# How far apart the loads of k, q and v are paced, from the third batch on

## The chip, the cores and the metric

The kernel runs on one core of one Trainium2 chip. The metric is the device time of one execution in microseconds. A core has a matmul engine (TensorE, PE in the profile, with its weight loads as PEld), VectorE (DVE), ScalarE (ACT), GpSimd (POOL) and SyncE (SP), which here only issues DMA transfers. Each engine runs its own list of instructions in order and waits on semaphores for the others. A DMA transfer is issued by one engine and carried out by 16 DMA engines that the core has to itself.

## The reference

Two blocks follow each other. The first is attention without a softmax, with a norm at the end; the second sends each token to one of eight experts.

```
# B, H, S, D = 8, 8, 576, 64
kv  = einsum('bhsd,bhse->bhde', k, v)
o   = einsum('bhsd,bhde->bhse', q, kv)
rms = sqrt(mean(o * o, axis=-1) + 1e-6)
x   = (o / rms * g_norm)  ->  (B*S, H*D) = (4608, 512)

# 8 experts, 576 tokens each
logits = x @ w_gate                      # (4608, 8)
# (token, expert) pairs by falling logit; a pair is taken if the token
# is still free and the expert not yet full
out[mask_e] = relu(x[mask_e] @ w1[e]) @ w2[e]     # w1 (512, 1024), w2 (1024, 512)
```

All inputs and the output are float32.

## The kernel before, in words

**Attention.** The work goes batch by batch, eight of them. k, v and q of a batch (576 rows of 64 for each of eight heads) are loaded in two halves each, so a batch has six loads of 576 KB, and the kernel has 48 in all. `load` (L82) makes a tile for one half, with a tag such as `k0` or `q1` that has two buffers, and hands the DMA to `paced`. A load of batch b + 2 therefore needs the buffer that batch b used, and waits until TensorE has read it for the last time.

`prepare(b)` (L368) turns a batch's loads into what attention needs. `sum_kv(r)` (L392) multiplies k with v for two heads at a time and adds up over the rows; `sum_kv(0)` and `sum_kv(1)` use the first halves of k and v, `sum_kv(2)` and `sum_kv(3)` the second. `turn_q(n)` (L376) transposes four blocks of q on TensorE; n = 0, 1, 2 use the first half of q, n = 2, 3, 4 the second. As soon as the last reader of a half has been written down, `again` (L399) writes down the load of the same half for batch b + 2.

`tiles` (L466) and its function `one` (L477) multiply the turned q with kv, 128 tokens at a time, take squares on ScalarE and sum them on VectorE. `logits` (L513) has GpSimd scale the tokens into `xo`, and collects writes of `xo` to a DRAM array `x_dram`, 20 of them, in the list `writes`.

The loop at L546 goes over the batches: between the output tiles of batch b it puts the pieces of `prepare(b + 1)`. Batches with an odd number have five output tiles, the others four. On TensorE, VectorE, ScalarE and SyncE the order is the order written down (`manual_schedule`, L542), so SyncE's list is: the 12 loads of the first two batches (L91), then the loads of the later ones as `again` writes them down, then the writes. The writes of the first six batches come after all the loads, at the ends of rounds 4 and 5 of the loop. The others follow after the last round; their `xo` is made by ScalarE in a list called `late`.

**Pacing.** `paced` (L74) keeps a list of all DMAs it has been handed, loads and writes together, numbered here from 0: 0 to 5 are the first batch's, 12 to 17 the third's, 42 to 47 the eighth's, 48 to 67 the writes. It adds a dependency to each: the DMA waits until the one three places ahead of it in this list has landed.

**Routing and experts.** After attention, VectorE and TensorE search for the thresholds that fill the first expert (`threshold`, L653). SyncE then reads the expert's number (L905), loads its weights (L911, L913), and GpSimd gathers its tokens from `x_dram` (L966). `turn` (L1047) and `layers` (L1090) do the matrix products, and the searches for later experts run beside them.

Of the kernel before, what the change touches and what calls it, by code (L numbers as in the profile page):

```python
# [26 lines left out]
def kernel(  # L27
# [14 lines left out]
    B, H, S, D = q.shape  # L42
# [25 lines left out]


    loaded = {}  # L70
    AHEAD = 3
    issued = []

    def paced(dma):  # L74

        if len(issued) >= AHEAD:
            tc.add_manual_dep(dma.ins, issued[-AHEAD].name,
                              mybir.DependencyInfo(mybir.DependencyClass.Sync, mybir.DependencyReason.DATA),
                              reason="paced loads")
        issued.append(dma.ins)  # L80

    def load(name, b, h):  # L82

        loaded[name, b, h] = att.tile([P, NP // 2, R, D], FT, name=f"{name}_sb", tag=name + str(h), bufs=2)
        rs = slice(h * NP // 2, (h + 1) * NP // 2)
        src = {"k": k, "v": v, "q": q}[name]
        paced(nc.sync.dma_start(
            loaded[name, b, h].rearrange("p r j d -> p r (j d)"),
            src[b].rearrange("h s d -> (h s) d").rearrange("(r p j) d -> p r (j d)", r=NP, j=R)[:, rs]))
# [138 lines left out]
    for st in range(1, NSTEP):  # L228
        n = (1.0 + 2 * FUZZ) / (NCAND + 1) if 1 < st <= DIGITS else 1.0 / (NCAND + 1)
# [4 lines left out]
    for st in range(1, NSTEP):  # L234
        n = (1.0 + 2 * FUZZ) / (NCAND + 1) if st <= DIGITS else 1.0 / (NCAND + 1)
# [230 lines left out]
    def tiles(c0, rows):  # L466
# [46 lines left out]
        def logits():  # L513

            part = att.tile([P, T * H, E], FT, name="part", tag="part")
            nc.vector.tensor_tensor(
                part, o_sb[:, :, :, D:W].rearrange("p t h e -> p (t h) e"),
                inv.rearrange("p (a o) -> p a o", o=1).to_broadcast([P, T * H, E]), op=AL.mult)
            nc.vector.reduce_sum(out=lg[:, :, c0:c0 + T].rearrange("p e t -> p t e"),
                                 in_=part.rearrange("p (t h) e -> p t e h", t=T), axis=AXX)  # L520

            for t in range(T):
                if own:
                    nc.gpsimd.tensor_tensor(xo[:, t], o_sb[:, t, :, 0:D],  # L524
                                            inv[:, t * H:(t + 1) * H].rearrange("p (h o) -> p h o", o=1).to_broadcast([P, H, D]),
                                            op=AL.mult)
                else:
                    for h in range(H):
                        late.append(lambda t=t, h=h: nc.scalar.mul(xo[:, t, h], o_sb[:, t, h, 0:D],
                                                                   inv[:, t * H + h:t * H + h + 1]))  # L530
            for x in range(0, T, 2):
                y = min(x + 2, T)
                writes.append(lambda x=x, y=y: paced(nc.sync.dma_start(
                    x_dram[(c0 + x) * P:(c0 + y) * P, :].rearrange("(t p) f -> p t f", p=P),
                    xo[:, x:y].rearrange("p t h d -> p t (h d)"))))
# [55 lines left out]
    for nm, shape in (("row", (NCAND + 1,)), ("cut", (2, GC)), ("mx", (GC,)), ("code_mx", (GC,)), ("mine", (GC,)),  # L591
                      ("shut", (E,)), ("code", (E,)), ("one_more", (3,)), ("marks", (NCAND // 2,)), ("which", (1,)), ("over_room", (E,)), ("last", (E,)), ("last_one", (1,)), ("begin", (1,)), ("half", (NB,)),
                      ("rise", (2, GC))):
        n = shape[0] * (shape[1] if len(shape) > 1 else 1)
# [6 lines left out]
    for nm, shape in (("n", (E, G)), ("all", (3, E)), ("a", (GC + 2,)), ("s", (NB, GC + 3))):  # L601
        n = shape[0] * (shape[1] if len(shape) > 1 else 1)
# [737 lines left out]
```

## Time and profile before

| | us |
|---|---|
| median of 3 runs | 644.92 (644.12 to 647.33) |
| profiled execution | 645.28 |
| its span, first to last instruction | 643.5 |
| TensorE busy | 600.3 (93%) |
| VectorE busy | 379.4 (59%) |
| GpSimd busy | 385.4 (60%) |
| ScalarE busy | 201.6 (31%) |
| first expert's weight load issued | 139.83 |

Times inside the profile are counted from the span's start. A row of the timeline gives start, duration, engine, line, operation, the tiles written and read, and how many instructions were merged; what stands in brackets is the idle time of the engine before it and what ended it. "issue" there means that the engine waited for nothing that the profile shows. The engine names with a q at the end, such as SPq, are sequencers: what they show of a DMA is its issue, not its travel. Queue 1 in the DMA table carries SyncE's transfers, queue 0 GpSimd's gathers and scatters, and queues 8 and 14 are of kind "instruction". The granted clock is the share of TensorE's full clock that the chip allowed in a stretch of time.

Attention takes about the first 106 us, the search for the first expert runs to about 140, and the eight experts fill the rest. DMA moves 305 GB/s between 20 and 94 us.

### The profile page before, as it was taken

Reading aid. Unit: us, or ns where it says so; the run is one execution under the profiler, and the core shown is the slowest. Engines: PE = TensorE matmul, PEld = TensorE weight load, DVE = VectorE, ACT = ScalarE, POOL = GpSimd, SP = SyncE. Lnnn points to the kernel's source line nnn. Section 1 sums busy time; section 2 is a strip of 40 time slices with the busy share of each in tenths; the row PEclk is TensorE's granted clock in tenths of the full one; section 3 lists DMA queues with packets and bytes.
Section 4 is the critical chain, followed back from the end, with each engine's and each line's share of the span. In section 5 each row is a group of like instructions: output and inputs, shape, how many; then the busy total and the mean of one; then the engine's idle time right before and its main releaser. Section 6 shows DMA issues by size and latency. Waiting matters only on the chain.

```text
span 643.5 us, 12772 instructions
## 1 busy us (share of the span) xinstructions
PE 600.3 (93%) x4914; PEld 465.6 (72%) x4924; DVE 379.4 (59%) x1242; ACT 201.6 (31%) x429; POOL 385.4 (60%) x402
## 2 busy tenths in 40 slices
PE   8889998348999999999999999999999999999994
PEld 4778887325787778677867786778678777867873
DVE  4457768776796778489658857966661062032101
ACT  1556666913221232213122312231232213122310
POOL 1136534005865697489729873887498579749822
PEclk9989999559999999999999999999999999999998
DMA  8899999438018107210911181027105410910001
GB/s 270 293 305 301 306 318 359 168 116 263 7 49 303 58 2 280 89 42 1 329 39 42 42 295 41 34 77 259 58 17 167 179 63 1 325 51 34 1 10 65
DMA packets 49853, 91.03 MB, mean 141 GB/s; under 512 B 3712, under 2 KB 20096, under 8 KB 49792
## 3 DMA queue, kind: packets, MB, share of 16 engines
q1 hardware_dynamic: 43200, 71.31, 32.4%
q0 software_dynamic: 5888, 18.88, 8.6%
q8 instruction: 39, 0.64, 0.4%
q14 instruction: 22, 0.18, 0.1%
q10 hardware_dynamic: 704, 0.02, 0.1%
HBM read 71.32 MB, written 18.87 MB: 140 GB/s over the span
## 4 chain that ended last, share of the span: by engine, by line
PE 79%; DVE 7%; issue 5%; DMA 4%; ACT 2%; POOL 1%; POOLq 0%; SPq 0%; DVEq 0%; ACTq 0%
PE x_ps L1156 13%; PE x_ps L1116 12%; PE z_ps L1156 9%; PE y_ps L1156 9%; PE y_ps L1116 8%; PE z_ps L1116 7%; PE o_ps L492 5%; PE y_ps L1218 4%; DMA v_sb<-in_v_dram 3%; PE qt_ps L381 3%; PE t_ps L1058 3%; PE kv_ps L396 2%; PE given_ps L670 1%; DMA q_sb<-in_q_dram 1%; PE given_ps L665 1%
## 5 line engine op out<-in xcount | busy, mean ns | idle before, releaser
L1161 ACT COPY h<-x_ps 128x288 f32<-128x288 f32 x93 | 37.2, 400 | 166.1 <-PE x_ps L1156 159.8
L1156 PE MATMUL x_ps<-xs,sw 128*128 128x288 f32 x248 | 71.4, 409 | 0.4 <-DVE xs L1071 0.4
L1083 POOL DMA_INDIRECT out_dram<-y_sb,outs x32 | 31.4, 983 | 56.7 <-DVE y_sb L1254 41.1
L1116 PE MATMUL x_ps<-tw,sh 128*128 128x256 f32 x256 | 61.5, 384 | 0.0
L1156 PEld LDWEIGHTS x_ps<-xs,sw 128*128 128x128 f32 x248 | 46.1, 190 | 13.4 <-issue 1.0
L1063 ACT ACTIVATE xt<-t_ps,g_col 128x512 f32<-128x512 f32 (+3 forms) x41 | 25.8, 635 | 91.4 <-PE t_ps L1058 91.2
L1108 POOL TENSOR_TENSOR sh<-hid 128x512 f32<-128x512 f32 x32 | 40.6, 1270 | 19.8 <-ACT hid L1131 19.8
L1116 PEld LDWEIGHTS x_ps<-tw,sh 128*128 128x128 f32 x256 | 47.0, 190 | 7.0 <-issue 0.8
L1044 POOL TENSOR_TENSOR sw<-w_sb 128x256 f32<-128x256 f32 x64 | 46.7, 730 | 7.8 <-PE z_ps L1156 7.4
L1131 ACT ACTIVATE hid<-hid 128x576 f32<-128x576 f32 x64 | 43.8, 686 | 22.5 <-DVE hid L1170 12.5
L524 POOL TENSOR_TENSOR xo<-o_sb,inv 128x512 f32<-128x512 f32 x27 | 28.3, 1079 | 34.1 <-DVE inv L511 34.1
L966 POOL DMA_INDIRECT xg<-x_dram,ids x40 | 38.1, 952 | 15.6 <-issue 10.4
L1194 POOL TENSOR_TENSOR tw<-w_sb 128x512 f32<-128x512 f32 x32 | 40.0, 1270 | 6.8 <-DMA w_sb<-in_moe_w_dram 6.8
L492 PE MATMUL o_ps<-kvx,qt 64*128 64x72 f32 (+1 forms) x640 | 39.9, 272 | 2.7 <-ACT o_sb L499 1.6
L492 PEld LDWEIGHTS o_ps<-kvx,qt 64*128 64x128 f32 (+1 forms) x640 | 34.9, 178 | 8.2 <-issue 5.1
L1156 PE MATMUL z_ps<-xt,sw 128*128 128x288 f32 x128 | 38.0, 414 | 0.0
L1156 PE MATMUL x_ps<-xt,w_sb 128*128 128x288 f32 x124 | 37.3, 415 | 0.5 <-ACT xt L1063 0.5
L1156 PE MATMUL y_ps<-xt,w_sb 128*128 128x288 f32 x128 | 36.8, 408 | 0.0
L1156 PE MATMUL z_ps<-xs,sw 128*128 128x288 f32 x128 | 36.8, 409 | 0.0
L1156 PE MATMUL y_ps<-xs,w_sb 128*128 128x288 f32 x128 | 36.5, 407 | 0.0
L503 DVE TENSOR_REDUCE ms<-sq 128x8 f32<-128x512 f32 x36 | 24.5, 683 | 19.8 <-ACT sq L498 19.7
L1248 ACT COPY u<-x_ps 128x512 f32<-128x512 f32 x24 | 14.0, 584 | 66.3 <-PE x_ps L1116 52.6
(306 smaller groups left out, 1322.1 us busy)
## 6 DMA issues: line engine op xcount, KB each, us to landing
w_sb<-in_moe_w_dram SPq DMA_DIRECT2D x32, 512.0 KB, 5.3
w_sb<-in_moe_w_dram SPq DMA_DIRECT2D x8, 2048.0 KB, 13.1
k_sb<-in_k_dram SPq DMA_DIRECT2D x16, 576.0 KB, 5.8
v_sb<-in_v_dram SPq DMA_DIRECT2D x16, 576.0 KB, 5.6
q_sb<-in_q_dram SPq DMA_DIRECT2D x16, 576.0 KB, 6.1
x_dram<-xo SPq DMA_DIRECT2D x16, 512.0 KB, 4.1
x_dram<-xo SPq DMA_DIRECT2D x4, 256.0 KB, 2.9
xg<-x_dram,ids POOLq DMA_INDIRECT x40, 5.2
```

The lines of the kernel that those rows point to most:

```text
L492: nc.tensor.matmul(o_ps[rows_at, rp, (2 * r2 + l) * W:(2 * r2 + l + 1) * W], lhsT=turned_q[bn][ks, l, block // 2:block // 2 + m].rearrange ...
L524: nc.gpsimd.tensor_tensor(xo[:, t], o_sb[:, t, :, 0:D], inv[:, t * H:(t + 1) * H].rearrange("p (h o) -> p h o", o=1).to_broadcast([P, H, D ...
L966: tokens = nc.gpsimd.indirect_dma_start(out=xg[0:nr], out_offset=None, in_=x_dram, in_offset=bass.IndirectOffsetOnAxis(ap=ids[0:nr, n:n + ...
L1044: in_order(nc.gpsimd.tensor_tensor(o, x, y, op=op))
L1063: nc.scalar.mul(xt[:, :, a + c:a + d], t_ps[:, :, c:d], g_col)
L1083: put = nc.gpsimd.indirect_dma_start(out=out, out_offset=bass.IndirectOffsetOnAxis(ap=ids_of[t][0:nr, n:n + 1], axis=0), in_=y_sb[0:nr, :] ...
L1108: in_order(nc.gpsimd.tensor_tensor(o[:, ms], x[:, ms], y[:, ms], op=op))
L1116: nc.tensor.matmul(p_ps[:, n], lhsT=left[:, f, n * P:(n + 1) * P], rhs=right[:, f], start=first, stop=(f == FH - 1), skip_group_check=True)
L1131: nc.scalar.activation(both, both, ACT.Relu)
L1156: nc.tensor.matmul(p_ps, lhsT=lhs[:, r], rhs=rhs[:, r], start=(m in (1, 2, 4, 5) and r == 0), stop=(r == 1), skip_group_check=(m in (6, 7, ...
L1161: nc.scalar.copy(u, p_ps)
L1194: in_order(nc.gpsimd.tensor_tensor(o, x, y, op=AL.subtract))
```

## The change

`paced` takes its distance from the place in the list. For numbers 12 to 47, the loads of the third to the eighth batch, it is six places; for the first 12 loads and for the writes it stays three.

```diff
     loaded = {}
-    AHEAD = 3
+    AHEAD, APIECE = 3, 6
     issued = []

     def paced(dma):

-        if len(issued) >= AHEAD:
-            tc.add_manual_dep(dma.ins, issued[-AHEAD].name,
+        n = APIECE if 2 * APIECE <= len(issued) < B * APIECE else AHEAD
+        if len(issued) >= n:
+            tc.add_manual_dep(dma.ins, issued[-n].name,
                               mybir.DependencyInfo(mybir.DependencyClass.Sync, mybir.DependencyReason.DATA),
                               reason="paced loads")
         issued.append(dma.ins)
```

Lines after this one have numbers that are one higher in the changed kernel.

## The prediction

> **What bounds the kernel now.** I read the page first (busy shares, the chain of waits), then TensorE's waits and timeline inside the attention stage, then SyncE's DMA issues, then the clock and the DMA rows stretch by stretch. The page's chain:
>
> ```profile
> span 643.5 us, 12772 instructions
> PE 79%; DVE 7%; issue 5%; DMA 4%; ACT 2%; POOL 1%; POOLq 0%; SPq 0%; DVEq 0%; ACTq 0%
> ```
>
> DMA has 4% of the chain, about 26 us, and the page puts three quarters of it on one v load group. The merged chain shows these pieces all before 26.3 us: loads of v at 1.25, 7.87 and 12.68, and a load of q at 19.24 that lands at 26.17. After that TensorE carries the chain through attention. So the question is what loads do to TensorE after about 21 us, where the changed loads begin. TensorE's waits from 18 to 110 us:
>
> ```profile
> PE kv_ps L396 <- issue: 3.9, 3, 1.6
> ...
> PE o_ps L492 <- issue: 0.7, 1, 0.7
> PE qt_ps L381 <- DMA q_sb<-in_q_dram: 0.2, 1, 0.2
> ```
>
> Columns are microseconds in total, times, longest. TensorE waits 0.2 us for a load and 4.6 us for "issue", that is for nothing the profile can name. Its timeline places these:
>
> ```profile
> 25.05 1.03 PE L396 MATMUL kv_ps<-v_sb,k_sb 64*64 64x64 f32 x47 [1.08 <-issue]
> 26.30 0.63 PE L381 MATMUL qt_ps<-ident,q_sb 128*128 128x128 f32 x4 [0.22 <-DMA q_sb<-in_q_dram]
> ...
> 37.84 1.70 PE L396 MATMUL kv_ps<-v_sb,k_sb 64*64 64x64 f32 x59 [1.56 <-issue]
> ...
> 61.89 0.67 PE L492 MATMUL o_ps<-kvx,qt 64*128 64x72 f32 x8 [0.66 <-issue]
> ...
> 84.80 0.35 PE L396 MATMUL kv_ps<-v_sb,k_sb 64*64 64x64 f32 x9 [1.28 <-issue]
> ```
>
> They fall in the middle of a run of matmuls on tiles already in use, and between the stops at 23.97 and 36.28 I count 252 matmul records, between 36.28 and 61.23 about twice that. This is the pace at which TensorE's instructions are fetched: queue 8 is of kind "instruction", 39 packets of 0.64 MB, 16 KB each, two to such a stretch. I take the stops for late instruction blocks. They are the only thing after 26.3 us that the loads could still change.
>
> The loads themselves, by SyncE's issues:
>
> ```profile
> 19.24 1.87 SPq L87 DMA_DIRECT2D q_sb<-in_q_dram  x2
> 22.68 0.37 SPq L87 DMA_DIRECT2D k_sb<-in_k_dram  x1
> 26.18 0.37 SPq L87 DMA_DIRECT2D v_sb<-in_v_dram  x1
> ...
> 30.70 3.45 SPq L87 DMA_DIRECT2D q_sb<-in_q_dram  x2
> 35.28 0.37 SPq L87 DMA_DIRECT2D k_sb<-in_k_dram  x1
> ...
> 93.53 37.42 SPq L533 DMA_DIRECT2D x_dram<-xo  x20
> ```
>
> Loads are numbered from 0 here, six to a batch. Load 12 (k of the third batch) goes at 22.68, load 18 at 35.28; each issue also shows that the load three places back has landed. So load 13 (v) had landed by 30.70 and is first read at 33.48, and load 15 (second half of v) had landed by 35.28 and is first read at 35.83: 0.55 us to spare, the thinnest margin. For later batches the same reading gives 3.4 to 6 us (fourth batch: v landed by 42.76, read at 49.09; eighth: landed by 88.92, read at 94.90). Loads are paced, but nobody waits for them.
>
> Clock and DMA by stretch (columns: busy time and count of the five engines, granted clock, DMA share, GB/s):
>
> ```profile
> 20.00:94.00 74.00, 67.18 (x1565) 58.46 (x1573) 46.91 (x140) 45.13 (x89) 30.55 (x34) 0.98 0.92 305
> 38.00:40.00 2.00, 2.00 (x62) 1.88 (x59) 0.00 (x0) 0.42 (x1) 0.13 (x1) 0.56 0.89 277
> ...
> 196.00:204.00 8.00, 8.00 (x47) 6.87 (x46) 5.25 (x19) 0.59 (x1) 6.58 (x8) 1.00 1.05 384
> ```
>
> **The change, part by part.** No instruction is added or removed, the order on every engine is the same, and on PE, ACT, DVE and POOL the waits are too. On SyncE the waits of 36 loads (12 to 47) move from three places back to six, and three writes behind them get an extra landing to wait for.
>
> 1. SyncE's own waits. Between 20 and 94 us it waits 56.4 us for landings (21.3 + 20.0 + 15.1) and 4.1 us for TensorE to free buffers. Most of the 56.4 goes and waits for buffers take its place. What is queued behind a waiting load is the next load, then 20 writes, then the weight loads, which need a routing result near 139.8 us. Nobody on the chain waits there: 0 us. What is late next is the buffer: each tile name has two buffers, so load 47 can't go before the sixth batch's last q tiles have been turned, about 81.6 us in the timeline.
>
> 2. A faster load stream. With up to 5 transfers queued (weights, 196 to 204 us, gathers beside them) the queues moved 384 GB/s at a share of 1.05, against 305 at 0.92 now. The 36 loads are 21.2 MB: 70 us at 305, 55 at 384; the buffers hold it to about 60. The last load goes at 82 to 86 us rather than 92. TensorE waits 0.2 us for loads in all, so the value is between 0 and -0.2 us; I take 0.
>
> 3. The q loads of the second batch. Loads 12, 13 and 14 no longer wait for a landing (the places six back, 6 to 8, had to land for 9 to 11) and their buffers are free by about 14 us; they go right behind load 11, at some 21.1 to 21.9 us instead of 22.68, 26.18 and 27.70. Load 10, the q load on the chain, is still on its way then. If they take bandwidth from it, 26.17 moves later, straight onto the chain. Ends: -0.2 us (the wait at 26.30 goes) and +3.5 us (one more of the largest gap between landings, 22.68 to 26.18). The nearest row is the five weight loads issued at 188.85 to 191.35: the small ones land in 6.2 us at the median, the large one in 15.6. The early ones were not held to the last one's time, so I take +0.3 us.
>
> 4. The late instruction blocks, 1.08 + 1.56 + 0.66 + 1.28 = 4.58 us, and the clock. After the 1.56 us stop the clock falls to 0.56 (38 to 40 us): 59 records take 1.70 us where 72 take 1.38 elsewhere (+0.57), four turns 1.11 instead of 0.66 (+0.45), an output tile 1.64 instead of 1.11 (+0.53), 1.55 us in all. Ends: the three stops after 26 us and the dip go, -(1.56 + 0.66 + 1.28 + 1.55) = -5.1 us; or refills stretch as the one in this row, from 21 to 24 us, did:
>
> ```profile
> q8 instruction: 1, 0.02, 4.8%
> ```
>
> There 4.8% of 16 engines times 3 us is 2.3 us for one 16 KB block, where other windows give 2.1%, 1.0 us. That is +1.3 us for each of three stops, +3.9. Which end? Two 3 us windows in the expert stage, one with the queues empty but for the block, one with them full:
>
> ```profile
> DMA packets 1, 0.02 MB, mean 5 GB/s; under 512 B 0, under 2 KB 0, under 8 KB 0
> ...
> q8 instruction: 1, 0.02, 2.3%
> ```
>
> ```profile
> DMA packets 467, 1.12 MB, mean 375 GB/s; under 512 B 40, under 2 KB 40, under 8 KB 466
> ...
> q8 instruction: 1, 0.02, 2.3%
> ```
>
> A block takes 1.1 us in both (231 to 234 and 255 to 258 us). The size of the queue beside it does not set its time, so the stops stay: 0 us.
>
> A rule that speaks against this change is in the Trainium skill, "DMA: Bandwidth & Descriptors", section on latency and other measured facts: access to HBM takes 0.2 us on average and 2 us under high load. If six loads in flight were the high load and three were not, each of the three late blocks would cost 1.8 us more, an estimate of +5.4 us from that page. The rows just shown do not have it: full and empty queues give the same block time.
>
> 5. The 20 writes start with the load stream's end, some 6 to 10 us earlier. The last five wait for ACT's late copies and the gathers for routing (first at 143.69 us), so the end stays: 0 us. Were that cover gone, the cost would be a landing, 4.1 us at the median.
>
> Sum: 0 + 0 + 0.3 + 0 + 0 = +0.3 us. The profiled execution took 645.28 us (span 643.5 and 1.8 around it), 0.36 above the median of the three runs, 644.92. Against the median: 645.2 us. Half a percent, 3.2 us, is about what a measurement of this kernel can tell from no change; the three runs lie that far apart.
>
> **The rivals.**
> Slower: a deeper queue delays instruction blocks, at the stops of 36, 61 and 84 us. For it: the 2.3 us block at 21.42, while loads were in flight. Against it: the pair of windows above. Price +1.3 us for each stop, and 1.55 us if one more of them makes the clock fall: +3.9 to +5.5, 649 to 651 us. It decides from the third stretched block (or two and a dip, 4.2 us) on.
> Faster: from about 45 us the loads wait for buffers, queues run empty between them, blocks come sooner. For it: a stop of 1.56 us only just cost the clock, so a slightly shorter one saves the 1.55 us as well. Against it: a block takes 1.1 us even alone. Price -3.1 us (36 us stop with its dip) to -5.1: 640 to 642 us. It needs the dip to go.
> Nothing moves: the stream is held by something other than the pace and still runs at 305 GB/s; the last load stays near 92 us. For it: a share of 0.92 leaves little. Against it: 384 GB/s later. Time 644.9, inside the forecast.
>
> **How the numbers follow.** Forecast (within 3.2 us of before, the third rival included) 0.57; slower by refills or by the q load of step 3 0.23; faster 0.20. The slower side gets more since step 3 can only add. The range goes from the faster rival's lower price, 640, to the slower's upper, 651, since each tail holds about 2 in 10; the likeliest case's own range is 642 to 648. Chances: faster 0.20, within 0.57, slower 0.23.
>
> **What would show it.** Step 1: SyncE's waits for landings fall below 25 us between 20 and 94 us and waits on PE grow. Step 2: the last load goes before 87 us, with 330 GB/s or more from 21 to 45 us. Step 3: the turn after the second batch's kv sums starts at 26.3 to 26.6 us. Step 4: 3 to 5 "issue" stops on TensorE, 3.5 to 5.5 us together, at the same matmul counts. Step 5: writes start at 84 to 88 us and end near 131. The prediction is wrong if TensorE's stops vanish or double, if a clock dip comes or goes, or if the routing after 106 us shifts by more than attention did.

## The result and the profile after

The changed kernel is slower: a ratio of 1.0076 to the kernel before, 95% interval 1.0048 to 1.0104. The ratio leaves out executions more than 1.5% above the fastest of their kernel, two of the changed kernel's 17, so it is not the quotient of the medians that follow. The median of 17 executions is 651.31 us, that of the kernel before 646.58 us in the same comparison, 4.7 us less. The profiled execution of the changed kernel took 648.27 us, with a span of 646.5 us against 643.5 before.

The page's span and chain, after:

```profile
span 646.5 us, 12770 instructions
PE 77%; DVE 9%; issue 6%; DMA 4%; POOL 1%; ACT 1%; POOLq 0%; SPq 0%; DVEq 0%; ACTq 0%
```

"issue" grew from 5% to 6% of the chain. These rounded shares of the whole span do not say where: up to 108 us the chain holds about 1.5 us more of it than before. TensorE's waits from 18 to 110 us, after (microseconds in total, times, longest):

```profile
PE kv_ps L397 <- issue: 4.8, 3, 2.5
PE o_ps L493 <- issue: 1.4, 2, 1.1
PE kv_ps L457 <- issue: 0.6, 1, 0.6
```

No wait for a load is left in this list. The "issue" waits at the kv sums (L397) and output tiles (L493) went from 4.6 to 6.2 us. TensorE's timeline, after, at the same instructions as those shown of before:

```profile
24.32 1.03 PE L397 MATMUL kv_ps<-v_sb,k_sb 64*64 64x64 f32 x47 [0.26 <-issue]
25.50 0.63 PE L382 MATMUL qt_ps<-ident,q_sb 128*128 128x128 f32 x4
...
38.03 1.59 PE L397 MATMUL kv_ps<-v_sb,k_sb 64*64 64x64 f32 x59 [2.48 <-issue]
...
42.94 1.97 PE L382 MATMUL qt_ps<-ident,q_sb 128*128 128x128 f32 x8
...
64.09 0.67 PE L493 MATMUL o_ps<-kvx,qt 64*128 64x72 f32 x8 [1.08 <-issue]
...
87.03 0.35 PE L397 MATMUL kv_ps<-v_sb,k_sb 64*64 64x64 f32 x9 [2.10 <-issue]
```

The stops are at the same records: after 25, 13, 8 and 60 matmuls of the same groups. The one near 24 us is shorter (0.26 for 1.08), the other three are longer by 0.92, 0.42 and 0.82 us. That is 5.9 us for the four, 4.6 before; the rest of the 6.2 is a wait of 0.36 us at 45.26, while the clock is low. The eight turns at 42.94 take 1.97 us, where they take 1.09 at full clock. The clock after the long stop, and DMA over the stage, after:

```profile
20.00:94.00 74.00, 66.53 (x1530) 57.92 (x1535) 45.46 (x135) 43.37 (x86) 30.55 (x34) 0.95 0.96 340
...
38.00:40.00 2.00, 1.97 (x61) 1.85 (x62) 0.00 (x0) 0.34 (x1) 0.00 (x0) 0.64 1.05 389
40.00:42.00 2.00, 2.00 (x18) 1.67 (x16) 0.72 (x6) 0.83 (x2) 0.85 (x2) 0.50 1.08 398
42.00:44.00 2.00, 2.00 (x15) 1.88 (x14) 0.69 (x1) 1.37 (x3) 0.36 (x1) 0.50 1.03 381
```

From 25 to 45 us, before and after:

```profile
25.00:45.00 20.00, 17.73 (x363) 15.23 (x365) 11.57 (x53) 9.72 (x20) 6.61 (x8) 0.91 0.91 298
```

```profile
25.00:45.00 20.00, 16.99 (x313) 14.32 (x307) 11.08 (x48) 9.50 (x19) 6.60 (x8) 0.84 1.05 391
```

DMA moves 340 GB/s instead of 305 from 20 to 94 us, and 391 instead of 298 from 25 to 45. The clock's dip lasts about 7 us instead of 3.4. TensorE's first search matmul begins at 115.26 instead of 113.25 us, which is 2.0 of the 3.0 us by which the two spans differ. From there to the first weight load it is 26.6 us in both; the other 1.0 us is in the expert stage, and no experiment followed it.

SyncE's issues, after:

```profile
20.51 0.47 SPq L88 DMA_DIRECT2D k_sb<-in_k_dram  x1
21.02 0.77 SPq L88 DMA_DIRECT2D v_sb<-in_v_dram  x1
21.84 0.90 SPq L88 DMA_DIRECT2D k_sb<-in_k_dram  x1
...
80.13 3.27 SPq L88 DMA_DIRECT2D q_sb<-in_q_dram  x2
85.46 47.49 SPq L534 DMA_DIRECT2D x_dram<-xo  x20
```

Loads 12 to 14 go at 20.5 to 21.8 us and the last load by about 83. Up to 45 us the stream runs ahead; from 52 us on each load goes when its buffer comes free.

### The profile page after: what moved, and what is told of

Its sections match the earlier page's. It is cut to its first block, busy times and chain, and to the rows that moved or that the text cites. A ratio compares the mean times of both kernels' runs of the same rounds, so it can differ in the third digit from the quotient of the medians.

```text
span 646.5 us, 12770 instructions
## 1 busy us (share of the span) xinstructions
PE 601.2 (93%) x4914; PEld 466.7 (72%) x4924; DVE 380.2 (59%) x1242; ACT 201.6 (31%) x429; POOL 385.5 (60%) x402
## 4 chain that ended last, share of the span: by engine, by line
PE 77%; DVE 9%; issue 6%; DMA 4%; POOL 1%; ACT 1%; POOLq 0%; SPq 0%; DVEq 0%; ACTq 0%
PE x_ps L1157 13%; PE x_ps L1117 11%; PE z_ps L1157 9%; PE y_ps L1157 9%; PE y_ps L1117 8%; PE z_ps L1117 7%; PE o_ps L493 4%; PE y_ps L1219 4%; PE qt_ps L382 3%; PE t_ps L1059 3%; DMA v_sb<-in_v_dram 3%; PE kv_ps L397 2%; PE given_ps L671 1%; DMA q_sb<-in_q_dram 1%; PE given_ps L666 1%
## 5 line engine op out<-in xcount | busy, mean ns | idle before, releaser
L493 PE MATMUL o_ps<-kvx,qt 64*128 64x72 f32 (+1 forms) x640 | 40.3, 273 | 2.5 <-issue 1.4
L493 PEld LDWEIGHTS o_ps<-kvx,qt 64*128 64x128 f32 (+1 forms) x640 | 35.2, 180 | 8.2 <-issue 5.8
L504 DVE TENSOR_REDUCE ms<-sq 128x8 f32<-128x512 f32 x36 | 24.4, 683 | 21.9 <-ACT sq L499 21.8
```

The source lines that it names most:

```text
L493: nc.tensor.matmul(o_ps[rows_at, rp, (2 * r2 + l) * W:(2 * r2 + l + 1) * W], lhsT=turned_q[bn][ks, l, block // 2:block // 2 + m].rearrange ...
```

## The experiments

Three theories stood at the start. A: the load stream makes TensorE's next instruction block come late, and more so with six loads ahead. B: the loss comes from the later batches, whose loads now wait for buffers. C: the clock dips fall by chance and the loads have no part in it.

**Half of the change each.** The condition on the number in the list is cut:

```diff
-        n = APIECE if 2 * APIECE <= len(issued) < B * APIECE else AHEAD
+        n = APIECE if 2 * APIECE <= len(issued) < 4 * APIECE else AHEAD   # early_six
+        n = APIECE if 4 * APIECE <= len(issued) < B * APIECE else AHEAD   # late_six
```

> Six places ahead for the loads of the third and fourth batch only (12 to 23), three for all others. Theory A (a deeper queue of loads makes TensorE's next instruction block start later, and the stop near 36 us with the clock dip behind it grows): nearly all of the loss is here, 3 to 5 us slower than before, a stop of 2.2 to 2.7 us near 36 us and a dip of two clock windows (6.8 us). Theory B (the loss comes from the later batches, whose loads now wait for buffers and are issued in bursts tied to TensorE): 0 to 1 us slower, the 36 us stop back near 1.6 us. Theory C (the clock dips fall by chance and the queue has no part in it): within 2 us of before, and the stop near 36 us is anything from 1.2 to 2.6 us.

> The other half: three places ahead up to load 23, six for loads 24 to 47 (fifth to eighth batch). Theory A: the stop near 36 us is 1.4 to 1.7 us with one clock window at half as before; the stops near 62 and 85 us grow by 0.3 to 0.8 us as in the changed kernel only if many loads are in flight then; 0 to 1.5 us slower than before. Theory B: 3 to 5 us slower, with the growth in the stops near 62 and 85 us. Theory C: within 2 us of before.

Measured: the early half alone 1.0067 (1.0042 to 1.0091) of before, median 648.85 us; the late half alone 1.0056 (1.0034 to 1.0079), 648.29 us. Each half costs nearly what both cost, so A and B as worded both fall short: the late half was to cost 0 to 1.5 us by A and the early half 0 to 1 by B. The traces give a part of the reason. With the late half alone the stream runs ahead at 43 to 67 us instead, and there the stop near 60 us is 1.75 us, against 0.66 and 1.21 in two profiles of before. The profile of the early half alone is of its longest execution, 656.91 us, so it does not show where the median's loss lies. Its long stop is the one near 24 us:

```profile
26.28 1.75 PE L397 MATMUL kv_ps<-v_sb,k_sb 64*64 64x64 f32 x47 [2.23 <-issue]
27.96 1.11 PE L382 MATMUL qt_ps<-ident,q_sb 128*128 128x128 f32 x4
```

The windows of the same profile (busy time and count of the five engines, clock, DMA share, GB/s):

```profile
28.00:42.00 14.00, 14.00 (x151) 10.83 (x154) 7.20 (x32) 5.90 (x12) 3.04 (x4) 0.50 1.05 391
```

The clock stays at half for 14 us and more, with TensorE never idle. What follows one stop can cost far more than the stop. The 16 KB instruction block that ends this one travelled 2.75 us, against about 1.0 for most; near 36 us, with TensorE at half clock and 391 GB/s moving, there was no stop at all.

**The stops are instruction blocks.** The 18 warm-up matmuls at the start become 36 of half the width, with six ahead and with three:

```diff
-        ones(18)
+        ones(36, width=256)
```

(`ones` gets a parameter for the width in both kernels; its lines are left out here.)

> The changed kernel, with the 18 warm-up matmuls at the start split into 36 of half the width: the same time on TensorE, 36 instructions more. If the stops are late instruction blocks (theory A and B), every stop moves forward by 18 matmul records in TensorE's order: the one near 36 us from record 13 of the second half's kv sums to the output tile before it, where matmuls take three times as long, so it shrinks from 2.5 to about 1.5 to 2.0 us; the one near 85 us from record 60 of the first half's sums to record 42 and stays near 2 us. The time falls by 0 to 3 us against the changed kernel. Theory C, or stops that come from data or semaphores: they stay at the same matmuls.

> The kernel before with the same split of the warm-up matmuls. Theories A and B: the stop near 36 us moves into the output tile ahead of the second half's kv sums and shrinks from 1.56 to 0.5 to 1.2 us, too short to cost the clock a window, so the dip (1.55 us) goes as well: 1 to 3 us faster than before. Theory C: stops at the same matmuls and no change.

Measured: 1.0025 (0.9999 to 1.0052), 647.04 us with six; 0.9986 (0.9951 to 1.0022), 644.91 us with three. The stops moved as counted. With six ahead:

```profile
24.49 1.27 PE L397 MATMUL kv_ps<-v_sb,k_sb 64*64 64x64 f32 x65 [0.62 <-issue]
...
34.23 0.89 PE L493 MATMUL o_ps<-kvx,qt 64*128 64x72 f32 x11
37.83 0.71 PE L493 MATMUL o_ps<-kvx,qt 64*128 64x72 f32 x5 [2.71 <-issue]
```

and with three:

```profile
34.12 0.89 PE L492 MATMUL o_ps<-kvx,qt 64*128 64x72 f32 x11
36.37 0.45 PE L492 MATMUL o_ps<-kvx,qt 64*128 64x72 f32 x5 [1.37 <-issue]
```

65 records are left at the first stop where 47 were, and the second stop falls after 11 of the 16 records of the output tile, 18 records ahead of where it was. Later stops moved by 18 as well: the one near 61 us (1.14 us with three ahead, 0.18 with six), and with three ahead also one at 65.60 and one at 88.02 us, which lie 18 records ahead of stops at 70.09 us in the third profile of the changed kernel and at 94.13 us in the second of before; with six there is one at 96.42, at the same instruction as the one at 88.02. The one expected near 85 us is in neither profile. A wait for data or a semaphore would have stayed with its instruction, so the places are set by the count of TensorE's instructions.

The DMA records of the traces say the same. Between 20 and 100 us the 17 profiles of this document have 67 stops marked "issue" of 0.2 us or more, and 63 of them end 1.2 to 1.55 us after a 16 KB block of queue 8 has landed. The other four are of 0.36 us each, while the clock is at half.

The sizes were not as expected: 2.71 us with six (1.5 to 2.0 expected), 1.37 with three (0.5 to 1.2), and with three ahead the time did not fall by the 1 to 3 us expected. At the same place, six ahead costs 1.34 us more, in one profile each; the one with six is of that kernel's longest execution, 654.32 us.

**No load stream.** The third and later batches use the tiles of the first two again:

```diff
+    kept = dict(loaded)
...
-                    load(name, b + 2, h)
+                    loaded[name, b + 2, h] = kept[name, b % 2, h]
```

> The kernel before without its loads 12 to 47: the third and later batches use the first two batches' k, q and v again, so what is computed from them is other data. Nothing else is left out. Theory A (the queue of loads delays instruction blocks): with almost empty queues from about 25 us on, the stops near 36, 61 and 84 us fall to 0 to 0.6 us each, no clock window at half before 110 us, 4 to 7 us faster than before. Rival (an instruction block is late in a short stretch of matmuls whatever the queues do): stops of 1.0 to 1.6 us stay, 0 to 2 us faster.

Measured: 0.9904 (0.9876 to 0.9931), 639.19 us. TensorE's waits from 18 to 100 us:

```profile
PE kv_ps L457 <- issue: 0.6, 1, 0.6
PE kv_ps L397 <- issue: 0.5, 1, 0.5
PE qt_ps L382 <- DVE qt L386: 0.2, 1, 0.2
PE ones_ps L362 <- issue: 0.2, 1, 0.2
```

Both "issue" waits of half a microsecond are before 25 us, when the last of the 12 loads is still on its way. After that there is no stop up to 93 us, and the clock is not lowered before 104 us. This is theory A's expectation: the loads make the blocks late, with three ahead as well. Theory C is out in so far as it gives the loads no part: none of the 11 executions without them had a mean clock below 0.96, against 23 of 98 of the kernel before in the four later comparisons. Without the loads the kernel is about 6 us faster; it routes other data, so this is only roughly the price of the stops and dips.

**How far ahead.**

```diff
-        n = APIECE if 2 * APIECE <= len(issued) < B * APIECE else AHEAD
+        n = 4 if 2 * APIECE <= len(issued) < B * APIECE else AHEAD            # four
+        n = 2 * APIECE if 2 * APIECE <= len(issued) < B * APIECE else AHEAD   # twelve
+        n = 2 if 2 * APIECE <= len(issued) < B * APIECE else AHEAD            # two
```

> Four places ahead for loads 12 to 47. Theory A: the stop near 36 us between that of three places (1.56 and 1.87 in two profiles) and of six (2.48), 1 to 4 us slower than before. Rival (what matters is only whether the DMA engines run dry between loads, and four is enough to keep them busy): as bad as six, 4 to 5 us slower, 370 GB/s or more from 25 to 45 us.

> Twelve places ahead for loads 12 to 47; the buffers allow no more than about nine in flight. Theory A with the delay growing with the queue's length: stops of 2.5 to 4 us near 24 and 36 us, 5 to 9 us slower than before. Rival (the delay is set by the DMA engines being busy without a gap, not by how much is queued): as with six, 4 to 5 us slower.

> Two places ahead for loads 12 to 47. The load stream falls to 220 to 260 GB/s. Theory A: the instruction blocks come sooner, stops of 0 to 1 us; but the third batch had 0.55 us to spare and now arrives late, and TensorE waits for loads 3 to 12 us in all, so 2 to 10 us slower than before. If the stream still reaches 290 GB/s, 0 to 3 us faster.

Measured: four 1.0037 (0.9997 to 1.0078), 647.34 us; twelve 1.0035 (0.9994 to 1.0077), 647.85 us; two 1.0312 (1.025 to 1.0374), 665.55 us. The stop near 36 us is 1.97 us with four and 364 GB/s from 25 to 45 us, and 2.48 us with twelve and 390 GB/s, the same as with six. More queued than six adds nothing to the stop, so the delay does not grow with the queue's length once the engines run without a gap. In time, though, neither four nor twelve is clear of no change, and twelve, with the same stop as six, met neither of its expectations (4 to 9 us slower). Two starves TensorE (waits from 18 to 112 us):

```profile
PE kv_ps L397 <- DMA v_sb<-in_v_dram: 5.8, 3, 2.7
PE qt_ps L382 <- DMA q_sb<-in_q_dram: 2.9, 2, 1.6
PE kv_ps L397 <- issue: 1.1, 1, 1.1
PE o_ps L493 <- issue: 0.4, 1, 0.4
```

One stop for a block is left, of 1.1 us near 24 us, at 219 GB/s from 25 to 45, but 8.7 us of waits for loads take the others' place, and the clock is at half for 10 to 17 us behind three of them: 20 us slower, well above the 2 to 10 expected.

**More profiles of the two kernels**, unchanged.

> The kernel before, profiled a second time. Theory A (busy DMA engines delay TensorE's instruction blocks): the stop near 36 us again between 1.2 and 2.0 us, those near 61 and 84 us between 0.4 and 1.5, at the same matmuls. If the block of 2.3 us at 21.42 was a chance event, it is about 1 us here, the stop near 24 us is 0.3 to 0.7 us, and the wait for the q load at 26 us is gone or moved with it.

> The changed kernel, profiled a second time. Theory A: the stop near 24 or 36 us is 2.2 to 2.7 us and is followed by at least two clock windows (6.8 us) at half; 375 to 395 GB/s from 25 to 45 us. If the long stop of the first profile was chance, it is below 1.9 us here.

> The changed kernel, a third profile, for the spread of the stops and of the clock dips behind them: the same as for the second by theory A. Dips of 3 to 5 windows (10 to 17 us) turn up in some profiles, and the time goes with the number of windows at half, about 1.3 to 1.7 us for each.

Before again: 653.82 us in this one execution, stops of 0.33, 1.06, 1.21 and 1.20 us, with a dip of 17 us behind the third and one of 10 us behind the last. The last is not the one near 84 us, which is missing here, but at 94.13 us, one block further on. The q load is no longer waited for (its turn starts at 25.36 us), and the block ahead of the first stop travelled 1.08 us, where it took 2.31 in the first profile: the 1.08 us stop and the 26.30 us start of the first profile came from one slow block. After, second and third: 647.23 and 649.80 us, the stop near 36 us 2.42 and 2.43 us, 390 GB/s from 25 to 45 us in both. The long stop is thus in all three profiles of the changed kernel. Its dip is not: it was 7 us, none and 3.4 us long. The expectation of at least two windows at half failed in the second, where a stop of 2.42 us cost no clock at all. In the second there is also a wait of 1.12 us at 51.37 us that ends with a load, so with six ahead TensorE is not wholly free of such waits.

**Smaller and larger transfers.** Every load is cut into two transfers of half its size, with six of these in flight:

```diff
-        if len(issued) >= AHEAD:
-            tc.add_manual_dep(dma.ins, issued[-AHEAD].name,
+        n = 2 * AHEAD if len(issued) < 12 * B else AHEAD
+        if len(issued) >= n:
+            tc.add_manual_dep(dma.ins, issued[-n].name,
...
-        paced(nc.sync.dma_start(
-            loaded[name, b, h].rearrange("p r j d -> p r (j d)"),
+        for i in range(2):
+            paced(nc.sync.dma_start(
+                loaded[name, b, h].rearrange("p r j d -> p r (j d)")[:, i:i + 1],
...
```

> The kernel before with every load cut into two of half its size and six of these in flight, so the same bytes in flight as before and the number of transfers of the changed kernel; at the start only four are out before the first has landed. Theory A, with busy DMA engines as the cause: the stream from 25 to 45 us lies between 300 and 340 GB/s, the stop near 36 us between 1.4 and 2.0 us, 0 to 3 us slower than before. If the number of transfers counts, it behaves as the changed kernel: a stop of 2.4 us or more, 4 to 5 us slower.

Measured: 0.9935 (0.9906 to 0.9965), 640.61 us, faster than both kernels. Neither expectation fits. From 25 to 45 us:

```profile
25.00:45.00 20.00, 18.69 (x365) 15.32 (x365) 12.97 (x61) 11.99 (x25) 6.61 (x8) 1.00 1.00 347
```

The stream is faster than with three whole loads (347 GB/s against 298) and yet there are only two stops, 1.31 and 0.47 us, and no dip. That opened theory S, argued from this one profile: a block waits for the transfer its DMA engine is working on, so its delay goes with the size of one transfer. Three kernels followed: halves with twelve ahead, transfers of twice the size with two in flight, and halves from the third batch on only.

```diff
-        n = 2 * AHEAD if len(issued) < 12 * B else AHEAD
+        n = 2 * AHEAD if len(issued) < 24 else 4 * AHEAD if len(issued) < 12 * B else AHEAD      # halves_deep
+        n = 2 if 12 <= len(issued) < 30 else AHEAD     # wholes; b >= 2: one DMA for a batch's k, v or q
+        n = AHEAD if len(issued) < 15 or len(issued) >= 84 else 2 * AHEAD     # halves_late
+        for i in (slice(0, 2),) if b < 2 else (slice(0, 1), slice(1, 2)):     # halves_late
```

> Loads cut into halves, and from the third batch on twelve halves ahead (the bytes of six loads), of which eight at most are out at a time. Theory S (an instruction block waits for the transfer that its DMA engine is working on, so its delay goes with the size of one transfer, 288 KB here and 576 KB in the changed kernel): stops as with six halves, none above 1.5 us, no clock window at half before 100 us, 640 to 643 us, even though the queue is as full and the stream reaches 375 GB/s or more. Theory A (the delay comes from DMA engines busy without a gap): a stop of 2.0 to 2.5 us near 24 or 36 us, 646 to 650 us.

> From the third batch on one load of 1152 KB for a batch's k, one for its v, one for its q, two in flight (the bytes of four loads before). The first two batches are loaded as before. Theory S: stops of 2.5 to 4.5 us at the instruction blocks, with dips of the clock behind them, 650 to 665 us, apart from waits of TensorE for loads, which the trace shows by name. Theory A: as with four loads ahead, stops of 1.8 to 2.0 us and 645 to 650 us.

> Loads of the first two batches as before; halves only from the third batch on, six halves ahead, that is as far ahead in bytes as before. Theory S: the gain of the halves is mostly kept, 639 to 643 us, one or two stops of 1.3 us or less after 30 us. If the gain of the halves came from the start (the first two batches), it is lost: 644 to 647 us.

Measured: halves with twelve ahead 0.9966 (0.9929 to 1.0003), 644.40 us; wholes 1.0015 (0.9964 to 1.0067), 651.73 us beside 648.22 for the kernel before in that comparison; late halves 0.9932 (0.9891 to 0.9972), 643.90 us. The stop of the deep halves:

```profile
36.02 1.60 PE L398 MATMUL kv_ps<-v_sb,k_sb 64*64 64x64 f32 x62 [2.13 <-issue]
```

2.13 us at 384 GB/s, as theory A has it, although each transfer is only half as large. The wholes had four stops of 1.08 to 1.85 us and one of 0.28 at 339 GB/s, not the 2.5 to 4.5 of S, and a wait of 1.11 us for a load. So the size of a transfer does not set the delay; the packets that the loads are made of were 2304 bytes in all these kernels, so these runs say nothing on their size. In time, the deep halves lie between the two expectations, 0.34% below the kernel before with an interval that just reaches it. The halves' gain does not lie in the first two batches, since the late halves keep it in their ratio, though not in their stops: 1.97 us near 36 us, where S allowed 1.3. Why the halves are faster is not settled: in the one profile of the late halves the named stops add up to 4.6 us, as before.

The stop near 36 us stands beside the stream from 25 to 45 us like this, one profile a row. The third column is how long before the stop's start the block that ends it begins to travel (the DMA records of the traces):

| loads | GB/s | block starts ahead of the stop, us | stop, us |
|---|---|---|---|
| none | 60 | about 3.0 | 0 |
| three ahead | 298 | 0.68 | 1.56 |
| three ahead, again | 318 | 1.30 | 1.06 |
| late half six ahead, three up to here | 302 | 0.52 | 1.87 |
| late halves | 307 | 0.46 | 1.97 |
| wholes, two ahead | 339 | 1.28 | 1.08 |
| halves | 347 | 0.97 | 1.31 |
| four ahead | 364 | 0.41 | 1.97 |
| halves, twelve ahead | 384 | 0.22 | 2.13 |
| six ahead | 391 | -0.04 | 2.48 |
| six ahead, again | 390 | 0.17 | 2.42 |
| six ahead, third | 390 | 0.12 | 2.43 |
| twelve ahead | 390 | 0.00 | 2.48 |

In all rows with a stop the block travels 0.99 to 1.12 us, and TensorE goes on 1.24 to 1.48 us after it has landed. What varies is when the block starts: 3.0 us ahead without the loads, 0.5 to 1.3 with three ahead, and with six about when TensorE stops. (Without the loads nothing stops; TensorE passes that place at about 35.6 us, and the block starts at 32.60.) The rate alone orders this only in part: below 370 GB/s the stop scatters between 1.06 and 1.97 us, above 380 it is 2.1 to 2.5 in every profile that has it at this place. The changed kernel keeps the DMA engines without a gap (a share of 1.05) while TensorE's next block, a DMA transfer too, has yet to start. What holds the block back, the profile does not show: it has no record of when a block is asked for.

## Why the prediction was wrong

645.2 us was predicted with "within half a percent" as likeliest. The kernel is 0.76% slower, and its 651.31 us is just outside the range, which ended at 651.0. The sign lay with the slower rival, given 0.23.

- **What bounds the kernel.** Right: after 26 us no load is waited for in the kernel before, and the late instruction blocks are what the loads could change. The shifted kernels and the one without loads show it.
- **Step 1** was right: SyncE's waits for landings fell from 56.4 to 15.9 us between 20 and 94 us (6.1 + 5.5 + 4.3 at the loads), and those for TensorE's buffers rose from 4.1 to about 33. They cost nothing by themselves. The writes behind the loads wait for the same three landings as before (4.4 us, now 4.5); the extra landing that the prediction gave them does not exist, since their distance stays three.
- **Step 2** was right about the stream: the last load at about 83 us, and 378 GB/s from 21 to 45 us where 330 or more was asked for. Its value was put at 0 because TensorE does not wait for loads. The harm came with the fuller stream, and this was not carried over to step 4.
- **Step 3** was put at +0.3 us, and nothing shows that cost: load 12 did go at 20.5 us, and the turn began at 25.50, 25.60 and 26.06 us in three profiles, against 26.30 and 25.36 before. The 0.22 us wait for the q load is in none of the three.
- **Step 4 is the step that failed.** It set the change of the stops at 0, from a block that takes 1.1 us beside full queues and 1.1 beside empty ones. That row shows how long a block travels once it has started, not how long it waits to start. In the first profiles the three stops after 26 us grew by 2.2 us together, not by 0, and the dip by 3.4 us. The two DMA records around 35.6 us show the difference, in a window of 0.1 us. Before:

```profile
q1 hardware_dynamic: 13, 0.03, 79.4%
q8 instruction: 1, 0.02, 62.6%
```

After:

```profile
q1 hardware_dynamic: 17, 0.04, 103.2%
q8 instruction: 1, 0.02, 70.1%
```

The shares of 16 engines times 0.1 us give 1.00 and 1.12 us for the block, so its travel hardly changed. In both it starts between 35.55 and 35.65 us, but TensorE was 0.7 us further on in the changed kernel: it had stopped at 35.55 and not at 36.28. Against TensorE's work the block starts 0.72 us later (0.04 us after the stop instead of 0.68 ahead of it), and the stop is longer by 0.92: 0.72 for the start, 0.12 for the travel, 0.08 for the time from landing to the next matmul. The table above has the same for the other kernels. The expert stage, from which 0 was taken, was a poor place to look for a late start: the two blocks used lie 24 us apart (232 and 256 us), those of the attention stage 4 to 9 us, so a late start had more time to hide there. This reason is argued; no run tested it.
- **Step 5** was right: the writes start at 85.46 us and the first weight load goes 26.6 us after the first search matmul, as before.
- **The slower rival** had the place, and its price of 3.9 to 5.5 us holds the 4.7 us between the medians. The mechanism was wrong for the stops that it priced: in the first profile their blocks did not stretch (1.02 to 1.12 us, before 1.00 to 1.03), they started late. That the price fits is partly luck, since the stops grew by 2.2 us and not 3.9, and clock dips made up the rest. Stretched blocks do occur, with three ahead (2.31 us at 21.42 us, before) and with six (2.75 us ahead of the early half's stop of 2.23 us; 1.98 us ahead of a stop of 2.35 us near 61 us in the second profile of the changed kernel), but the runs do not tie them to the distance.
- **The dip** was counted as one window more, +1.55 us. It varies more widely than that. Of the 98 executions of the kernel before in the later comparisons, 23 had a mean clock below 0.96, and of the 17 of the changed kernel, 9. At 0.963 and above the medians are 645.0 and 648.20 us, 3.2 us apart; below 0.96 they are 652.24 and 654.11. So about two thirds of the loss are there without the longer dips, and the rest fits their being more frequent. That a longer stop makes a dip likelier fits this too, but no run set the length of a stop by itself, and the executions compared come from different comparisons. The mean clock is that of the whole span, and takes in a stretch of 31 to 38 us at half clock in the search, which is in every profile.
- **The faster rival** asked for shorter stops once loads wait for buffers. The stops near 62 and 85 us did not become shorter as a rule: 1.08 and 2.10, 2.35 and 0.55, 1.08 and 1.24 us in the three profiles of the changed kernel, against 0.66 and 1.28 in the first of before, and 1.21 and none in the second.
- The rule of the Trainium skill weighed in the prediction ("DMA: Bandwidth & Descriptors", section on latency and other measured facts: access to HBM goes from 0.2 us to 2 us under high load) pointed the right way, and the argument against it rested on the same row as step 4. That its estimate, +5.4 us, is near the 4.7 us measured is luck: it was for three stops, and these grew by 2.2 us. What the runs show is a late start; no run here shows how long an access to HBM takes.

## What to carry to other kernels

A transfer that nobody waits for can still cost time, because blocks of instructions are DMA transfers as well: look for idle time marked "issue" in the middle of a run of small matmuls, count the records between such stops, and test by adding a few instructions at the start to see whether the stops move. For such a stage the pace of loads has to be found between the waits for data (two ahead: 665.55 us) and the late blocks (six ahead: 651.31 us). Of the whole loads three ahead was best here, though four and twelve are not clearly worse. It is not simply the slowest stream that arrives in time: the halves ran at 347 GB/s and beat three whole loads at 298. Whether a resource is hidden has to be read from when a thing starts against the work that needs it, not from how long it takes once it runs.

## What the runs showed of the hardware that was not expected

- A stop of 2.23 us, ending at 26.28 us, was followed by 16 us at half clock with TensorE busy throughout, and one of 2.42 us by no dip at all.
- Queueing beyond six loads changed neither the stream (390 GB/s) nor the stop (2.48 us).
- Without loads 12 to 47 the kernel takes 0.9904 of the time before, and with all loads cut in halves 0.9935: about two thirds of what the loads cost can be had back, and the reason for the halves' gain is open.
